# Chunked attention and two MLPs on one core: q, k and softmax weights transposed by DMA as 16-bit halves

## The chip, the cores and the metric

The kernel runs on one core of a Trainium2 chip. The metric is the device time of one execution in microseconds (us); lower is better. The core has a matrix engine (TensorE, PE in the profile; its weight loads are PEld), a vector engine (VectorE, DVE), a scalar engine (ScalarE, ACT), GpSimd (POOL) and SyncE (SP), which here issues nearly all DMAs. Each engine works through its own instructions in order and waits on semaphores for the others.

## The reference

Attention within chunks of 64 tokens for 4 batches of 8 heads (576 tokens, head size 64), then two MLPs over the 2304 tokens of width 512: one with a leaky activation (2048 hidden) and one bilinear (1536 hidden). All is float32.

```python
scores = scale * np.matmul(q_c, k_c.transpose(0, 1, 2, 4, 3))   # per chunk of 64
scores = scores - np.max(scores, axis=-1, keepdims=True)
attn = np.exp(scores)
attn = attn / (np.sum(attn, axis=-1, keepdims=True) + 1e-09)
out = np.matmul(attn, v_c)                     # then x: (2304, 512)
h = x @ w_in
x = (np.maximum(h, 0.0) + alpha * np.minimum(h, 0.0)) @ w_out
out = ((x @ w_a) * (x @ w_b)) @ w_o
```

## The kernel before, in words

Attention works on 18 groups of 128 tokens (two chunks, eight heads). A group's q, k and v are loaded with tokens on the partitions and 512 columns (`load`, L202). PE multiplies over the partitions, so k and q are first transposed by PE into PSUM, four 128x128 pieces each, and copied by ACT to the tiles kT and qT (`att_T`, L232 and L234). 32 small matmuls make the scores (`att_S`, L245). DVE subtracts the maximum (`att_M`, L258 and L260), ACT takes the exponential (`att_X`, L266), DVE divides by the sum (`att_N`, L271 to L275); the weights are in tile e. PE transposes e as well (`att_PT`, L281), ACT copies it to eT (L283), and 32 matmuls with v give the output (`att_O`, L293), which ACT and DVE split into a high and a low part, xh and xl, the first MLP's input.

Each product of the MLPs is made from such halves in three matmuls (`three`, L317). Tokens go through the first MLP in five blocks: block 0 of 512 tokens (groups 0 to 3), block 1 of 256 (groups 4 and 5), blocks 2 to 4 of 512 (groups 6 to 9, 10 to 13, 14 to 17). A block has 16 steps j: 12 matmuls into psh, the activation (`prelu`, L331: neg and pos on ACT, pos on DVE, gh on ACT, gl on DVE), and, two steps later, 12 matmuls into the accumulators acc. In block 0 the weights are also loaded, unpacked and split on ACT and DVE. The second MLP follows, block by block.

The attention of the groups of block b + 1 runs inside block b. `att_steps` (L459) gives it as a list of (slot, step); slot 2j comes between the matmuls into psh of step j and its activation, slot 2j + 1 at the end of step j (`advance` and `settle`, L600 to L633). So the attention of groups 4 and 5 runs in block 0, that of 6 to 9 in block 1, that of 10 to 13 in block 2, and that of 14 to 17 in block 3. For each block but block 1's own groups, step `turn(w)` transposes k and q of its group w, issues the loads of the next group's k and q, and transposes e of group w - 1; `multiply(w)` makes the scores of group w and the outputs of group w - 1; `soften(w)` is the exponential and the division. The steps are spread evenly over the slots.

Order is as written: every engine's instructions are issued in program order (a schedule by hand). Tiles come from pools: 72 shared tiles of 2 KB per partition (wp), 64 of which hold the first MLP's weights from block 1 on, three staging tiles of 4 KB (stg), and four PSUM banks each for accumulators and for the rest. A tile's next writer waits for the last reader of what it held.

Of the kernel before, what the change touches and what calls it, by code (L numbers as in the profile page):

```python
# [8 lines left out]
F32 = mybir.dt.float32  # L9
F32R = mybir.dt.float32r  # L10
I32 = mybir.dt.int32
U16 = mybir.dt.uint16
AF = mybir.ActivationFunctionType
# [5 lines left out]
def chunk_attention_prelu_mlp_bilinear_mlp(  # L19
# [17 lines left out]
    nc = tc.nc  # L37
    P = 128
    B, H, S, D = q.shape
    NT, DM = out.shape  # L40
# [5 lines left out]
    KD = DM // P  # L46
    J1 = F1 // P
    J2 = F2 // P
    NB = 512
    SCALE = 1.0 / float(D) ** 0.5  # L50

    sizes = [NB] + ([NT % NB] if NT % NB else []) + [NB] * (NT // NB - 1)
# [9 lines left out]
    sp = ctx.enter_context(tc.tile_pool(name="sp", bufs=3))  # L62
    st = ctx.enter_context(tc.tile_pool(name="st", bufs=4))
    dr = ctx.enter_context(tc.tile_pool(name="dr", bufs=1, space=bass.MemoryType.DRAM))
# [3 lines left out]
    def bank(nm="ps"):  # L68
        return ps_p.tile([P, DM], F32, tag="ps", name=nm)
# [5 lines left out]
    def wtile(name, dt=F32R):  # L75
        return wp.tile([P, DM], dt, tag="w", name=name)
# [88 lines left out]
    def weave(*chains):  # L165


        live, later = [], [iter(c) for c in chains]
        while live or later:
            if later:  # L170
                live.append(later.pop(0))
            live = [c for c in live if next(c, None) is not None]
# [16 lines left out]
    att = {}  # L189

    def runs(t, n):
        done = 0
        while done < n:
            b, s = divmod(t + done, S)
            step = min(n - done, S - s)
            yield done, step, b, s
            done += step

    def half(i):
        return slice(i * CH, (i + 1) * CH)  # L200

    def load(nm, u):  # L202
        a = att[nm, u] = wtile(f"{nm}{u}", F32)
        for off, n, b, s in runs(u * P, P):
            nc.sync.dma_start(
                out=a[off:off + n].rearrange("p (h d) -> p h d", h=H),
                in_={"q": q, "k": k, "v": v}[nm][b, :, s:s + n, :].rearrange("h p d -> p h d"),
            )

    def load_qk(u):  # L210
        load("k", u)
        load("q", u)

    def load_v(u):
        load("v", u)

    n_early = [0]

    def att_bank(u, nm):

        if u < sizes[0] // P:
            n_early[0] += 1
            if n_early[0] % 2:
                return acc_p.tile([P, DM], F32, tag="acc", name=nm)
        return bank(nm)

    def att_T(u, nms="kq"):
        for nm in nms:
            src = att.pop((nm, u))
            ps = att_bank(u, "psT")  # L230
            for g in range(KD):
                nc.tensor.transpose(ps[:, g * P:(g + 1) * P], src[:, g * P:(g + 1) * P], ident)  # L232
            t = wtile(f"{nm}T{u}", F32)
            nc.scalar.activation(out=t, in_=ps, func=AF.Copy)  # L234
            att[nm + "T", u] = lambda r, g, c, t=t: t[r, half(2 * g + c)]

    def att_S(u, pss=None):
        qT, kT = att.pop(("qT", u)), att.pop(("kT", u))
        pss = pss or [att_bank(u, "psS") for _ in range(2)]
        for y in range(2):  # L240
            for c in range(2):
                for e in range(2):
                    for x in (e, 1 - e):
                        i = half(e), 2 * x + y, c
                        nc.tensor.matmul(  # L245
                            out=pss[e][half(x), half(2 * y + c)], lhsT=qT(*i), rhs=kT(*i),
                            start=True, stop=True,
                        )
        att["s", u] = pss
# [15 lines left out]
    def att_X(u):  # L265
        nc.scalar.activation(out=att["e", u], in_=att["e", u], func=AF.Exp, scale=SCALE)  # L266
# [9 lines left out]

    def att_PT(u):
        e_ = att.pop(("e", u))
        ps = att_bank(u, "psP")
        for g in range(KD):  # L280
            nc.tensor.transpose(ps[:, g * P:(g + 1) * P], e_[:, g * P:(g + 1) * P], ident)  # L281
        t = wtile(f"eT{u}", F32)
        nc.scalar.activation(out=t, in_=ps, func=AF.Copy)  # L283
        att["eT", u] = t

    def att_O(u, xh, xl, col, pss=None):
        eT, v_ = att.pop(("eT", u)), att.pop(("v", u))
        pss = pss or [att_bank(u, "psO") for _ in range(2)]
        for g in range(KD):
            x, y = divmod(g, 2)  # L290
            for c in range(2):
                for e in (c, 1 - c):
                    nc.tensor.matmul(  # L293
                        out=pss[c][half(e), half(g)], lhsT=v_[half(c), half(2 * g + e)],
                        rhs=eT[half(c), half(4 * e + 2 * y + x)], start=True, stop=True,
                    )
        cols = [slice(col + c * CH, col + (c + 1) * CH) for c in range(2)]
        return [
            (xh[:, :, f], xl[:, :, f], ps[:, :KD * CH].rearrange("p (g i) -> p g i", g=KD))
            for f, ps in zip(cols, pss)  # L300
        ]

    def each(fn, parts):
        for part in parts:
            fn(*part)
# [22 lines left out]
    def s1(j, x, n):  # L328
        return proj(W["i", j], x, n)[:, :n]
# [121 lines left out]
    NU = NT // P  # L451
# [7 lines left out]
    def att_steps(b, x):  # L459

        t0, n = blocks[b]
        us = range(t0 // P, (t0 + n) // P)

        def turn(w):
            for u in us[w:w + 1]:
                att_T(u)
                if u + 1 < NU:
                    load_qk(u + 1)  # L470
            for u in us[max(w - 1, 0):w]:
                att_PT(u)
            return lambda: None

        def multiply(w):
            pss = [bank("psSO") for _ in range(2)]
            now, before = us[w:w + 1], us[max(w - 1, 0):w]
            for u in now:
                att_S(u, [ps[:, :KD * CH] for ps in pss])
            o = []  # L480
            for u in before:
                o += att_O(u, *x, u * P - t0, [ps[:, KD * CH:] for ps in pss])
                if u + 2 < NU:
                    load_v(u + 2)
            each(to_hi, o)

            def then():
                for u in now:
                    att_M(u)
                each(to_lo, o)  # L490

            return then

        def soften(u):
            att_X(u)
            return lambda: weave(att_N(u))

        def both(product):
            pss = [bank("psSO") for _ in range(2)]
            return [product(u, [ps[:, i * KD * CH:(i + 1) * KD * CH] for ps in pss]) for i, u in enumerate(us)]  # L500

        def both_S():
            both(att_S)
            return lambda: att_M(us[0])

        def both_O():
            o = sum(both(lambda u, pss: att_O(u, *x, u * P - t0, pss)), [])
            each(to_hi, o)
            for u in us:
                load_v(u + 2)  # L510
            return lambda: each(to_lo, o)

        def only(fn):
            return lambda: fn() and None or (lambda: None)

        if b == 1:
            u0, u1 = us
            return [
                (8, only(lambda: att_T(u0))),
                (10, only(lambda: (att_T(u1), load_qk(u1 + 1)))),  # L520
                (14, both_S),
                (16, lambda: lambda: att_M(u1)),
                (18, lambda: soften(u0)),
                (20, lambda: soften(u1)),
                (24, only(lambda: [att_PT(u) for u in us])),
                (27, both_O),
            ]
        steps = []
        for w in range(len(us) + 1):
            steps += [lambda w=w: turn(w), lambda w=w: multiply(w)]  # L530
            steps += [lambda u=u: soften(u) for u in us[w:w + 1]]
        last = 2 * J1 - 3
        return [(-(-last * i // (len(steps) - 1)), s) for i, s in enumerate(steps)]

    with tc.manual_schedule():
        n0 = sizes[0] // P
# [12 lines left out]
        x = xtiles("x")  # L549
# [46 lines left out]
        for b, (t0, n) in enumerate(blocks):  # L596
            nxt = xtiles("x")
            steps = att_steps(b + 1, nxt) if b + 1 < NBLK else []
# [11 lines left out]
            for j in range(J1):  # L610
# [5 lines left out]
                h = h0[0][:, :n] if not (b or j) else s1(j, x, n)  # L616
                if b == 0:
                    g = prelu_unpacking(j, h, lambda: w_dma(min(2 * j + 9, NU1)), lambda: advance(2 * j), settle)
                else:
                    rest = advance(2 * j)  # L620
                    g = prelu(j, h)
# [17 lines left out]
            x = nxt  # L639
        flush(0)  # L640

        for i, b in enumerate(order2):
            n = sizes[b]
            for j in range(J2):
                want = NU1 + max(3 * (j + 2), 20 + 2 * j)
                c = s3(j, x, n)
# [14 lines left out]
                if i + 1 < NBLK:  # L661
                    if j == J2 - 3:
                        nxt = xtiles("y")
                        halves = list(reload(order2[i + 1]))
                    if j >= J2 - 2:
                        e = j - (J2 - 2)
                        resplit(2 * e, halves[e], nxt)
            x = nxt
# [31 lines left out]
```

## Time and profile before

| | us |
|---|---|
| median of 3 runs | 912.65 (912.55 to 913.15) |
| the profiled execution | 912.5 |
| its span | 910.7 |
| PE busy | 898.5 |
| DVE busy | 403.3 |
| ACT busy | 339.4 |

Busy times are sums over the span; the three engines overlap. A stretch is read by which engine is full in it, and the chain of waits tells which instruction each one followed. Block 1 begins near 117 us of the span, block 2 near 178, block 3 near 273, block 4 near 372; the second MLP takes the part after 460.

### The profile page before, as it was taken

The numbers are of one execution on the slowest core, as the hardware profiler recorded it, in microseconds if no ns is written. First come the engines' busy times: TensorE is split into PE (matmuls) and PEld (weight loads), VectorE is DVE, ScalarE is ACT, GpSimd is POOL, SyncE is SP. The second block draws the span as 40 slices with busy tenths as digits, with TensorE's granted clock in tenths as the row PEclk, the third lists the DMA queues.
The fourth block names the chain that finished last, engine by engine and source line by source line (L and its number), as shares of the span: only waits on it lengthen the run. The fifth ranks groups of instructions, "written<-read, shape, count | busy, mean of one in ns | idle before, by whom it ended". The sixth has DMA issues, their size and how long they took to land.

```text
span 910.7 us, 13047 instructions
## 1 busy us (share of the span) xinstructions
PE 898.5 (99%) x5426; PEld 756.9 (83%) x5426; DVE 403.3 (44%) x762; ACT 339.4 (37%) x636; POOL 0.7 (0%) x6
## 2 busy tenths in 40 slices
PE   7999999999999999999999999999999999999998
PEld 6878899988888888888888888888888888888897
DVE  5999955443444343368856653111221122111222
ACT  5677654443433343356644432111211122111211
POOL 0000000000000000000000000000000000000000
PEclk9999999999999999999999999999999999999999
DMA  8685432221111110154424420200020002000100
GB/s 209 207 262 179 140 100 52 59 59 35 36 36 59 35 24 2 44 187 139 139 70 140 134 74 13 80 0 1 1 93 1 0 1 70 1 1 0 47 2 23
DMA packets 89098, 62.70 MB, mean 69 GB/s; under 512 B 59856, under 2 KB 81872, under 8 KB 89040
## 3 DMA queue, kind: packets, MB, share of 16 engines
q1 hardware_dynamic: 88752, 61.62, 22.8%
q8 instruction: 42, 0.69, 0.3%
q10 hardware_dynamic: 288, 0.26, 0.1%
q14 instruction: 16, 0.13, 0.1%
HBM read 53.49 MB, written 8.39 MB: 68 GB/s over the span
## 4 chain that ended last, share of the span: by engine, by line
PE 92%; DVE 5%; ACT 2%; issue 1%; POOLq 0%; ACTq 0%; POOL 0%; DVEq 0%
PE psh L317 52%; PE acc L317 36%; PE psT L232 1%; DVE wx L136 1%; PE psSO L245 1%; PE psP L281 1%; PE psSO L293 1%; DVE wz L128 1%; DVE wz L133 1%; DVE gl L82 0%; DVE sm L271 0%; DVE e L275 0%; PE warm L555 0%; DVE e L260 0%; DVE mx L258 0%
## 5 line engine op out<-in xcount | busy, mean ns | idle before, releaser
L393 DVE TENSOR_TENSOR b_sb<-psh,b_sb 128x512 f32<-128x512 f32 (+1 forms) x60 | 38.3, 638 | 273.2 <-PE psh L317 273.2
L337 DVE SCALAR_TENSOR_TENSOR pos<-neg,nalpha_sb,pos 128x512 f32<-128x512 f32 (+1 forms) x80 | 55.6, 695 | 116.4 <-ACT pos L336 116.2
L391 ACT ACTIVATE b_sb<-psh 128x512 f32<-128x512 f32 (+1 forms) x60 | 33.1, 552 | 167.9 <-PE psh L317 167.9
L79 ACT ACTIVATE ch<-b_sb 128x512 fp32r<-128x512 f32 (+1 forms) x60 | 35.3, 589 | 153.9 <-DVE b_sb L393 153.9
L335 ACT ACTIVATE neg<-psh 128x512 f32<-128x512 f32 (+1 forms) x80 | 44.1, 551 | 79.0 <-PE psh L317 79.0
L82 DVE TENSOR_TENSOR gl<-pos,gh 128x512 fp32r<-128x512 f32 (+1 forms) x80 | 51.0, 638 | 43.5 <-ACT gh L79 43.5
L79 ACT ACTIVATE gh<-pos 128x512 fp32r<-128x512 f32 (+1 forms) x80 | 47.3, 591 | 61.5 <-DVE pos L337 61.5
L82 DVE TENSOR_TENSOR cl<-b_sb,ch 128x512 fp32r<-128x512 f32 (+1 forms) x60 | 38.3, 639 | 39.3 <-ACT ch L79 39.3
L136 DVE SCALAR_TENSOR_TENSOR wx<-wx,wz 128x512 int32<-128x512 int32 x68 | 46.8, 688 | 4.9 <-ACT wx L124 1.0
L336 ACT ACTIVATE pos<-psh 128x512 f32<-128x512 f32 (+1 forms) x80 | 44.2, 552 | 0.0
L124 ACT ACTIVATE wx<-raw 128x512 f32<-128x512 f32 x68 | 42.7, 670 | 3.5 <-DMA raw<-in_moe_w_b_dram 3.4
L128 DVE TENSOR_SCALAR wz<-raw 128x512 uint16<-128x512 uint16 x68 | 29.7, 461 | 2.6 <-DMA raw<-in_moe_w_b_dram 2.6
L133 DVE TENSOR_SCALAR wz<-raw 128x512 uint16<-128x512 uint16 x68 | 30.9, 454 | 0.0
L234 ACT ACTIVATE kT<-psT 128x512 f32<-128x512 f32 x18 | 10.7, 594 | 20.1 <-PE psT L232 20.1
L79 ACT ACTIVATE xh<-psSO 128x256 fp32r<-128x256 f32 x28 | 9.1, 381 | 17.1 <-PE psSO L293 17.1
L266 ACT ACTIVATE e<-e 128x512 f32<-128x512 f32 x18 | 11.2, 623 | 10.4 <-DVE e L260 10.4
L281 PE MATMUL psP<-ident,e 128*128 128x128 f32 x72 | 11.6, 287 | 3.3 <-ACT eT L283 1.7
L258 DVE TENSOR_REDUCE mx<-psSO 128x4 f32<-128x256 f32 x28 | 10.5, 416 | 5.2 <-ACT xh L79 5.2
L275 DVE TENSOR_TENSOR e<-e,rc 128x512 f32<-128x512 f32 x18 | 12.4, 691 | 0.6
L271 DVE TENSOR_REDUCE sm<-e 128x8 f32<-128x512 f32 x18 | 12.2, 680 | 1.0 <-ACT e L266 0.8
L281 PEld LDWEIGHTS psP<-ident,e 128*128 128x128 f32 x72 | 8.5, 145 | 4.9 <-ACT eT L283 1.8
L232 PE MATMUL psT<-ident,q 128*128 128x128 f32 x72 | 11.2, 280 | 1.3 <-issue 1.3
(729 smaller groups left out, 2535.4 us busy)
## 6 DMA issues: line engine op xcount, KB each, us to landing
raw<-in_moe_w_out_dram SPq DMA_DIRECT2D x28, 512.0 KB, 3.5
raw<-in_moe_w_in_dram SPq DMA_DIRECT2D x16, 512.0 KB, 4.8
raw<-in_moe_w_b_dram SPq DMA_DIRECT2D x12, 512.0 KB, 4.9
raw<-in_moe_w_a_dram SPq DMA_DIRECT2D x12, 512.0 KB, 3.5
k<-in_k_dram SPq DMA_DIRECT2D x16, 256.0 KB, 3.8
q<-in_q_dram SPq DMA_DIRECT2D x16, 256.0 KB, 3.2
v<-in_v_dram SPq DMA_DIRECT2D x16, 256.0 KB, 3.3
out_dram<-os SPq DMA_DIRECT2D x8, 512.0 KB, 2.8
```

The lines of the kernel that those rows point to most:

```text
L79: nc.scalar.activation(out=hi, in_=src, func=AF.Copy)
L82: nc.vector.tensor_tensor(out=lo, in0=src, in1=hi.bitcast(F32), op=ALU.subtract)
L124: return nc.scalar.activation(out=x.bitcast(F32), in_=hw.bitcast(F32), func=AF.Copy, scale=2.0 ** -112)
L128: yield nc.vector.tensor_scalar(out=z2[:, :, 0], in0=h2[:, :, 1], scalar1=13, scalar2=None, op0=ALU.logical_shift_right)
L133: yield nc.vector.tensor_scalar(out=z2[:, :, 1], in0=h2[:, :, 3], scalar1=1 << 15, scalar2=None, op0=ALU.bitwise_and)
L136: yield nc.vector.scalar_tensor_tensor(out=x, in0=x, scalar=3, in1=z, op0=ALU.logical_shift_left, op1=ALU.bitwise_or)
L317: nc.tensor.matmul(out=ps, lhsT=a, rhs=b, start=(i == 0 and first), stop=(i == n_i - 1 and a is wl))
L335: nc.scalar.activation(out=neg, in_=h, func=AF.Relu, scale=-1.0)
L336: yield nc.scalar.activation(out=pos, in_=h, func=AF.Relu)
L337: yield nc.vector.scalar_tensor_tensor(out=pos, in0=neg, scalar=nalpha_sb[:, j:j + 1], in1=pos, op0=ALU.mult, op1=ALU.add)
L391: nc.scalar.activation(out=b_sb, in_=pb, func=AF.Copy)
L393: nc.vector.tensor_tensor(out=b_sb, in0=pa, in1=b_sb, op=ALU.mult)
```

## The change

For groups 6 to 17 k and q no longer go to PE to be transposed. `load_kq` loads both (into one staging tile, except for group 6). `apart` has ACT copy each with its 32-bit values taken apart: 512 low halves of 16 bits, then 512 high halves on each partition; and a DMA writes these to a DRAM tile, so that DRAM holds 256 rows of 512 halves, two for each token (`halves`). `turn_qk` issues a DMA that transposes the 256 rows back into a tile of 128 partitions (`turned`). The low and high half of one value come to lie side by side, so the tile is kT or qT in 32 bits. For groups 10 to 17 the softmax weights take the same way in `att_PT`, in one go: ACT's copy, the DMA to DRAM, the transposing DMA. All these DMAs are issued by SP.

The slots are now written out in tables: `m` the products, `s` the softmax, `p` the weights' transposes, `l`, `a`, `t` the loads, the taking apart and the transposes of k and q of a group further on. In block 1 outputs follow one group behind the scores, as before; in blocks 2 and 3 two groups behind, the last two groups' outputs in one step. The groups 0 to 5 keep PE's transposes.

```diff
--- before.py
+++ after.py
@@ -211,8 +211,54 @@
         load("k", u)
         load("q", u)

+    def pair(nm, staged):
+
+        if not staged:
+            return [wtile(nm, F32) for _ in range(2)]
+        a = sp.tile([P, 2, DM], F32, tag="stg", name=nm)
+        return [a[:, i] for i in range(2)]
+
+    def load_kq(u, staged=True):
+        att["kq", u] = a = pair(f"kq{u}", staged)
+        for off, n, b, s in runs(u * P, P):
+            for i, src in enumerate((k, q)):
+                nc.sync.dma_start(
+                    out=a[i][off:off + n].rearrange("p (h d) -> p h d", h=H),
+                    in_=src[b, :, s:s + n, :].rearrange("h p d -> p h d"),
+                )
+
     def load_v(u):
         load("v", u)
+
+
+
+
+
+    P_DMA = 10
+
+    def halves(src, dst, nm):
+
+        d = dst.bitcast(U16).rearrange("p (t f) -> p t f", t=2)
+        nc.scalar.activation(out=d, in_=src.bitcast(U16).rearrange("p (f t) -> p t f", t=2), func=AF.Copy)
+        rows = dr.tile([P, 2, DM], U16, name=f"rows{nm}")
+        nc.sync.dma_start(out=rows, in_=d)
+        return rows
+
+    def turned(rows, nm):
+        t = wtile(nm, F32)
+        nc.sync.dma_start_transpose(
+            out=t.bitcast(U16).rearrange("p (g r) -> p g r", g=KD), in_=rows.rearrange("p t f -> (p t) f")
+        )
+        return t
+
+    def apart(u, staged=True):
+        a, d = att.pop(("kq", u)), pair("kqd", staged)
+        att["rows", u] = [halves(a[i], d[i], f"{nm}{u}") for i, nm in enumerate("kq")]
+
+    def turn_qk(u):
+        for nm, rows in zip("kq", att.pop(("rows", u))):
+            t = turned(rows, f"{nm}T{u}")
+            att[nm + "T", u] = lambda r, g, c, t=t: t[r, half(2 * g + c)]

     n_early = [0]

@@ -276,6 +322,9 @@

     def att_PT(u):
         e_ = att.pop(("e", u))
+        if u >= P_DMA:
+            att["eT", u] = turned(halves(e_, wtile(f"ed{u}", F32), f"e{u}"), f"eT{u}")
+            return
         ps = att_bank(u, "psP")
         for g in range(KD):
             nc.tensor.transpose(ps[:, g * P:(g + 1) * P], e_[:, g * P:(g + 1) * P], ident)
@@ -463,18 +512,9 @@
         t0, n = blocks[b]
         us = range(t0 // P, (t0 + n) // P)

-        def turn(w):
-            for u in us[w:w + 1]:
-                att_T(u)
-                if u + 1 < NU:
-                    load_qk(u + 1)
-            for u in us[max(w - 1, 0):w]:
-                att_PT(u)
-            return lambda: None
-
-        def multiply(w):
+        def multiply(w, lag):
             pss = [bank("psSO") for _ in range(2)]
-            now, before = us[w:w + 1], us[max(w - 1, 0):w]
+            now, before = us[w:w + 1], us[max(w - lag, 0):max(w - lag + 1, 0)]
             for u in now:
                 att_S(u, [ps[:, :KD * CH] for ps in pss])
             o = []
@@ -495,42 +535,72 @@
             att_X(u)
             return lambda: weave(att_N(u))

-        def both(product):
+        def both(product, us):
             pss = [bank("psSO") for _ in range(2)]
             return [product(u, [ps[:, i * KD * CH:(i + 1) * KD * CH] for ps in pss]) for i, u in enumerate(us)]

         def both_S():
-            both(att_S)
+            both(att_S, us)
             return lambda: att_M(us[0])

-        def both_O():
-            o = sum(both(lambda u, pss: att_O(u, *x, u * P - t0, pss)), [])
+        def both_O(us):
+            o = sum(both(lambda u, pss: att_O(u, *x, u * P - t0, pss), us), [])
             each(to_hi, o)
             for u in us:
-                load_v(u + 2)
+                if u + 2 < NU:
+                    load_v(u + 2)
             return lambda: each(to_lo, o)

-        def only(fn):
-            return lambda: fn() and None or (lambda: None)
+        def nothing():
+            pass
+
+        def only(fn, *a):
+            def step():
+                if a[0] < NU:
+                    fn(*a)
+                return nothing
+
+            return step

         if b == 1:
             u0, u1 = us
             return [
-                (8, only(lambda: att_T(u0))),
-                (10, only(lambda: (att_T(u1), load_qk(u1 + 1)))),
+                (8, only(att_T, u0)),
+                (10, only(att_T, u1)),
+                (10, only(load_kq, u1 + 1, False)),
                 (14, both_S),
                 (16, lambda: lambda: att_M(u1)),
                 (18, lambda: soften(u0)),
                 (20, lambda: soften(u1)),
-                (24, only(lambda: [att_PT(u) for u in us])),
-                (27, both_O),
+                (21, only(apart, u1 + 1, False)),
+                (24, only(att_PT, u0)),
+                (24, only(att_PT, u1)),
+                (24, only(turn_qk, u1 + 1)),
+                (25, only(load_kq, u1 + 2)),
+                (27, lambda: both_O(us)),
+                (28, only(apart, u1 + 2)),
+                (29, only(load_kq, u1 + 3)),
+                (30, only(turn_qk, u1 + 2)),
             ]
-        steps = []
-        for w in range(len(us) + 1):
-            steps += [lambda w=w: turn(w), lambda w=w: multiply(w)]
-            steps += [lambda u=u: soften(u) for u in us[w:w + 1]]
-        last = 2 * J1 - 3
-        return [(-(-last * i // (len(steps) - 1)), s) for i, s in enumerate(steps)]
+        u = us[0]
+        if sizes[b - 1] < NB:
+            S_, lag = {
+                "m": (0, 7, 14, 21, 28), "s": (2, 9, 16, 23), "p": (6, 13, 20, 27),
+                "l": ((4, 3), (11, 4), (18, 5), (29, 6)), "a": ((1, 2), (8, 3), (15, 4), (24, 5)), "t": ((4, 2), (11, 3), (25, 4), (29, 5)),
+            }, 1
+        else:
+            S_, lag = {
+                "m": (0, 6, 12, 18), "s": (2, 8, 14, 20), "p": (4, 10, 16, 22),
+                "l": ((3, 3), (9, 4), (15, 5), (24, 6)), "a": ((1, 2), (7, 3), (15, 4), (23, 5)), "t": ((3, 2), (13, 3), (21, 4), (29, 5)),
+            }, 2
+        steps = [(slot, lambda w=w: multiply(w, lag)) for w, slot in enumerate(S_["m"])]
+        steps += [(slot, lambda w=w: soften(us[w])) for w, slot in enumerate(S_["s"])]
+        steps += [(slot, only(att_PT, us[w])) for w, slot in enumerate(S_["p"])]
+        if lag == 2:
+            steps += [(28, lambda: both_O(us[-2:]))]
+        for i, fn in enumerate((load_kq, apart, turn_qk)):
+            steps += [(slot, only(fn, u + n)) for slot, n in S_["lat"[i]]]
+        return sorted(steps, key=lambda s: s[0])

     with tc.manual_schedule():
         n0 = sizes[0] // P
```

## Rows read from the trace of the kernel before

**Rows 1.** The page: busy us (share of the span) and instructions.
```profile
PE 898.5 (99%) x5426; PEld 756.9 (83%) x5426; DVE 403.3 (44%) x762; ACT 339.4 (37%) x636; POOL 0.7 (0%) x6
```
**Rows 2.** The page: the chain that ended last, by engine.
```profile
PE 92%; DVE 5%; ACT 2%; issue 1%; POOLq 0%; ACTq 0%; POOL 0%; DVEq 0%
```
**Rows 3.** Stretches: length, busy PE, PEld, DVE, ACT, POOL; granted clock, DMA share, GB/s.
```profile
90.00:100.00 10.00, 9.61 (x47) 7.89 (x46) 9.90 (x22) 5.49 (x11) 0.00 (x0) 1.00 0.42 132
117.00:178.00 61.00, 60.38 (x691) 57.56 (x690) 32.16 (x76) 30.69 (x78) 0.00 (x0) 1.00 0.32 78
178.00:276.00 98.00, 98.00 (x700) 81.30 (x699) 39.05 (x75) 38.90 (x74) 0.00 (x0) 1.00 0.16 39
276.00:374.00 98.00, 98.00 (x689) 80.79 (x688) 39.16 (x74) 39.32 (x74) 0.00 (x0) 1.00 0.11 28
```
**Rows 4.** PE's waits, 54 to 900 us: waited for, us in total, times, longest.
```profile
PE psP L281 <- DVE e L275: 0.7, 2, 0.4
...
PE psP L281 <- ACT kT L234: 0.3, 1, 0.3
```
**Rows 5.** The chain in order of time, block 3: start, us, what.
```profile
273.36 2.72 PE psh L317 x12
276.08 0.87 PE psT L232 x8
...
296.87 0.87 PE psT L232 x8
297.74 0.44 PE psP L281 x4
298.18 2.77 PE psh L317 x12
...
303.67 0.62 PE psSO L245 x32
304.29 0.47 PE psSO L293 x32
304.76 2.95 PE psh L317 x12
...
365.25 0.62 PE psSO L293 x32
...
371.55 2.72 PE psh L317 x12
```
**Rows 6.** The same view, blocks 0 and 1.
```profile
96.16 0.63 PE psP L281 x4
...
117.16 1.43 PE psh L317 x12
...
146.86 0.63 PE psP L281 x4
...
177.70 2.75 PE psh L317 x12
```
**Rows 7.** Groups of ACT's instructions by shape: count, busy us, mean ns, idle before.
```profile
L124 ACT ACTIVATE wx<-raw 128x512 f32<-128x512 f32 x68 | 42.7, 670 | 3.5 <-DMA raw<-in_moe_w_b_dram 3.4
L234 ACT ACTIVATE kT<-psT 128x512 f32<-128x512 f32 x18 | 10.7, 594 | 20.1 <-PE psT L232 20.1
L79 ACT ACTIVATE gh<-pos 128x256 fp32r<-128x256 f32 x16 | 6.7, 417 | 11.2 <-DVE pos L337 11.2
L79 ACT ACTIVATE yh<-xr 128x1024 fp32r<-128x1024 f32 x6 | 6.3, 1044 | 0.0
```
**Rows 8.** DMA: a queue's packets, MB, share of 16 engines; issues with median us to landing.
```profile
q1 hardware_dynamic: 88752, 61.62, 22.8%
...
k<-in_k_dram SPq DMA_DIRECT2D x16, 256.0 KB, 3.8
...
x2d<-xs SPq DMA_DIRECT2D x2, 256.0 KB, 2.3
```
**Rows 9.** SP's own waits: waited for, us in total, times, longest.
```profile
SPq L205 <- PE psT L232: 77.8, 8, 13.8
```

## What the change was forecast to do

> **What bounds the kernel now.** I read the page's busy times first. The reader is to see that TensorE (PE) is busy for 898.5 of the 910.7 us of the span [rows 1], and that the chain of work that ended last lies on PE for 92% of it [rows 2]. Then the table by stretch, cut near the starts of blocks 1 to 4: in the stretches of blocks 2 and 3 PE is busy for 98.00 of 98.00 us at the full clock, in that of block 1 for 60.38 of 61.00, while ScalarE (ACT) is at 30.7 to 39.3 us and VectorE (DVE) at 32.2 to 39.2 [rows 3]. Only the end of block 0 has a second engine at its limit: DVE 9.90 of 10.00 us, ACT 5.49 [rows 3]. What PE waits for in blocks 1 to 3 comes to 0.3 us for a copy of kT and some 0.3 of the 0.7 us for the softmax weights e [rows 4]. So a PE instruction taken out of blocks 1 to 3 shortens the kernel by its own spacing, as long as nothing else arrives later than PE does now.
>
> **What one group's transposes cost.** The chain in order of time shows block 3 piece by piece, without a gap [rows 5]: 12 matmuls take 2.72 us, the eight transposes of a group's k and q 0.87, the four of its softmax weights 0.44, the scores 0.62, the outputs 0.47 behind scores (0.62 alone), and the matmuls behind a product 2.95, which is 0.23 more. From 273.36 to 371.55 it is 98.19 us. Of this 32 x 2.72 = 87.04 are the block's own matmuls; 4 x 0.87 + 4 x 0.44 = 5.24 are transposes; 4 x 0.62 + 3 x 0.47 + 0.62 + 5 x 0.23 = 5.66 are the products. The rest, 0.25, is 0.05 behind each of five transposing places (2.77 for 2.72). So a transpose costs its spacing of 0.11 us.
>
> **The change part by part.**
>
> 1. *k and q of groups 6 to 17.* Twelve times eight transposes leave PE: 12 x 0.87 = 10.44 us. Four of these twelve stand in block 1 (groups 6 to 9), four in block 2, four in block 3.
>
> 2. *Softmax weights of groups 10 to 17.* Eight times four: 8 x 0.44 = 3.52 us. Those of groups 6 to 9 stay on PE in block 1. Three of these four take 0.61 to 0.63 there already (one row stands), and the one that now follows k and q at 0.44 will begin by itself, so I charge 0.17 [rows 6].
>
> 3. *What goes with them.* The 0.05 behind ten transposing places in blocks 2 and 3 is 0.5; with block 1, where some places stay, I take 0.4. Of the 0.6 us that PE waits in block 1, the 0.3 for kT has no cause left; the wait for e is DVE's, and I leave it. Sum: 10.44 + 3.52 + 0.4 + 0.3 - 0.17 = 14.5 us.
>
> 4. *Outputs two groups behind the scores.* In blocks 2 and 3 the same products are made: four scores and four outputs in five places, the last now with two outputs (0.62 + 0.47). 0 us; PE's places only change.
>
> 5. *Copies on ACT.* 24 + 8 evacuations of 0.59 to 0.60 us go, 19.1 us. 32 copies of 1024 halves per partition come. No row has one; the nearest in element count is the 128x1024 copy at 1.04 us, so 33.4 us in all [rows 7]. The lower bound is a 512-element copy, 0.59; the upper is twice the strided copy of the weights, 2 x 0.67 = 1.34. Net +14 us on ACT, spread over blocks 0 to 3. In block 1 it means 8 x 1.04 - 8 x 0.59 = +3.6 on 30.7 of some 57 us. Each pair of copies stands ahead of a prelu and holds it for 2.1 us. PE multiplies by that prelu's result two steps later: four runs of 12 matmuls, 5.8 us in block 1 (1.44 each) and 10.9 in the other blocks, against the prelu's own five steps, of which gh at 256 columns takes 0.42 [rows 7], so some 2.3 with their hand-overs (an estimate). Cover left in block 1: 5.8 - 2.3 - 2.1 = 1.4 us. 0 us; gone, it costs up to 0.7 per group (at 1.34 each with an exp beside). In block 0 the pair for group 6 stands where DVE is full; ACT there has 4.5 of 10 us free, so 0 to 0.5, and I take 0.
>
> 6. *DMAs on SP's queue.* Per operand: the rows go out (256 KB; 2.3 us for the store of that size) and come back transposed. No row shows a transposing DMA. The nearest row by bytes is the load of k, 256 KB in 3.8 us [rows 8]. The other end follows from how finely it is cut: the queue's 88752 packets took 22.8% of 16 engines' 910.7 us, which is 37 ns each. If the 131072 halves of one operand moved in pieces of 32, 4096 pieces on 16 engines would take 9.6 us; one by one, 306 us. I take 3.8, since its pieces (256 bytes) are nearest to the 512-byte run that one destination partition receives per block of columns.
>
> 7. *The new waits.* SP waits for ACT's copy, then for the rows to have landed, before it issues a transpose. Behind it stand the next loads of k, q and v and the stores of x2d. Before, these loads stood behind PE as well, 77.8 us in total, because 64 of the 72 shared tiles hold weights [rows 9]. My count of the 8 others in program order peaks at 8 after the change too, so SP should wait no longer for a tile; the untransposed k and q move to the three staging tiles. PE waits for a transposed pair at its scores. The tightest distances: group 10, from slot 25 of block 1 to slot 0 of block 2, 7 slots; a slot there lasts (177.70 - 117.16) / 32 = 1.9 us now [rows 6] and 1.76 after, so 12.3 us. In block 2 group 13 has 5 slots of 2.9, 14.5 us. Two transposes of 3.8 need 7.6. The weights' round trip has at least 8 slots, 23 us, against 1.0 + 2.3 + 3.8 = 7.1. So hidden: 0 us. The cover is gone above some 6 us a transpose.
>
> [...]
>
> **The rivals.** *A, the transposes are the bound (slower).* They share the 16 DMA engines, so what counts is the sum. The first is issued at slot 24 of block 0, about 96 us [rows 6]; the last is needed at the outputs of group 17, some 351 us after the change (365 less 14) [rows 5]. 32 transposes in 255 us is 8 us each at best; with the distances above it decides from about 6. In pieces of 32 halves they take 32 x 9.6 = 307 us, 52 more than there is: 898 + 52 = 950 us. [...] Against: a destination partition gets 512 contiguous bytes at a time, and DMA is idle for most of these blocks (shares 0.11 to 0.32) [rows 3].
>
> *B, block 1 is too short.* Its slots are the shortest. The load of k and q of group 9 has slots 4 to 8, about 8 us, and waits first for the rows of group 8 to leave the staging tile and shares the engines with two stores of x2d. ACT waits for it in order, ahead of a prelu with 1.4 us of cover. At 2 us lost for each of groups 8 to 11, and as much again at the pairs of copies at 1.34, 4 x 2 = 8 us come back: 906 us. For it: the load's 3.8 us, 2.3 of the rows and the copies make 8.2. Against: the buffer is asked for only by SP, and ACT is half idle.
>
> *C, no change.* The time PE saves is waited elsewhere, DVE in block 1 for instance. DVE is at 32.2 of 61.0 us there, and PE would have to wait 14 us: 911 us. Little speaks for it.
>
> **How the numbers follow.** The profiled execution took 912.5 us with a span of 910.7, so 1.8 lie around it; the median of the runs, 912.65, is 0.15 above. 910.7 - 14.5 + 1.8 + 0.15 = 898.1, so I forecast 898.0. Chances: forecast (897 to 901) 0.70, B (901 to 909) 0.16, C 0.04, A 0.10. The low end takes in that all 0.7 us of PE's waits for e go and the 0.17 isn't paid, with 0.3 for the runs' spread: 898.0 - 1.2 = 896.8. The high end, 906, reaches to the price of B and leaves out A, C and a little of B. The measurement can tell about 0.2% (1.8 us) from no change: faster 0.86, same 0.04, slower 0.10.
>
> **What would show it.** Right: block 3 takes 98.2 - 5.4 = 92.8 us from its first psh to the next block's, block 2 loses as much, and block 1 lasts about 57; 48 transposes of k and q and 40 of weights remain on PE; a copy of halves takes near 1.04 us; a transpose lands within 6 us of its issue; PE's waits on kT, qT and eT come to under 1 us. Wrong, A: PE idles in blocks 1 to 3 until a DMA of kT, qT or eT, and the DMA share there is near 1. Wrong, B: PE waits for gl in block 1 while ACT waits for a load of kq or for a staging tile. What would make the whole prediction wrong is that time per transposing DMA, which no row gives.

## The result and the profile after

The changed kernel takes 897.67 us (median of 4 runs, 897.18 to 898.17) against 912.6 before: a ratio of 0.9835 (95% interval 0.9823 to 0.9848), 15 us or 1.6% less. Beside the experiments it ran twice more, at 897.79 and 897.59. The span of the profiled execution falls from 910.7 to 895.8.

The first part of the page, its DMA queue and its DMA issues, and the group of ACT's new copies (they answer to rows 1, 8 and 7):

```profile
PE 884.1 (99%) x5298; PEld 743.9 (83%) x5298; DVE 402.7 (45%) x762; ACT 352.6 (39%) x636; POOL 0.7 (0%) x6
...
L242 ACT ACTIVATE kqd<-kq 128x1024 uint16<-128x1024 uint16 x24 | 23.9, 1047 | 0.3 <-DMA kq<-in_k_dram 0.3
...
q1 hardware_dynamic: 127152, 78.41, 31.0%
...
rowsk<-kqd SPq DMA_DIRECT2D x12, 256.0 KB, 2.1
...
kT<-rowsk SPq DMA_TRANSPOSE x12, 4.0
qT<-rowsq SPq DMA_TRANSPOSE x12, 3.5
eT<-rowse SPq DMA_TRANSPOSE x8, 3.2
```

PE has 128 instructions fewer (5426 - 5298 = 96 + 32) and is busy 14.4 us less; it is still the full engine. ACT has as many as before and is busy 13.2 us more. A transposing DMA lands 3.2 to 4.0 us after its issue, by the medians of the three groups.

The waits of PE between 54 and 900 us (answers to rows 4), then the stretches from the first psh of blocks 1, 2 and 3 to that of the next (answers to rows 3; same columns):

```profile
PE psT L278 <- ACT pos L385: 0.6, 1, 0.6
PE psP L330 <- DVE e L321: 0.4, 1, 0.4
```
```profile
117.30:173.38 56.08, 56.08 (x657) 53.94 (x657) 32.00 (x76) 33.32 (x78) 0.00 (x0) 1.00 0.72 172
173.38:263.98 90.60, 90.47 (x642) 74.15 (x641) 38.17 (x75) 44.17 (x75) 0.00 (x0) 1.00 0.47 113
263.98:356.68 92.70, 92.70 (x641) 75.87 (x641) 38.91 (x75) 40.62 (x70) 0.00 (x0) 1.00 0.26 69
```

PE waits for no DMA at all; both waits that this view lists are in block 0. The DMA share of block 1 went from 0.32 [rows 3] to 0.72. The chain in order of time (answers to rows 5 and 6), start, us, what:

```profile
117.30 1.43 PE psh L366 x12
...
131.00 0.44 PE psP L330 x4
...
173.38 2.76 PE psh L366 x12
...
186.31 0.43 DVE xs L459
...
186.78 1.66 PE acc L366 x6
...
263.98 2.72 PE psh L366 x12
...
347.20 1.09 PE psSO L342 x64
...
356.68 2.72 PE psh L366 x12
```

The reader is to see that block 3 is products and matmuls alone, that the weights' transposes that stay in block 1 cost 0.44 each, and that at 186 us PE's chain runs over DVE's copy xs, which before it did not. From the first psh of each block to that of the next (before from rows 5 and 6):

| us | before | after | difference |
|---|---|---|---|
| block 1 | 60.54 | 56.08 | -4.46 |
| block 2 | 95.66 | 90.60 | -5.06 |
| block 3 | 98.19 | 92.70 | -5.49 |

With block 0 longer by 0.14 that is -14.87, the whole difference of the spans (14.9).

### The profile page after: what moved, and what is told of

Same layout as the page of the kernel before. It is cut to its first block, busy times and chain, and to the rows that moved or that the text cites. A ratio compares the mean times of both kernels' runs of the same rounds, so it can differ in the third digit from the quotient of the medians.

```text
span 895.8 us, 12893 instructions
## 1 busy us (share of the span) xinstructions
PE 884.1 (99%) x5298; PEld 743.9 (83%) x5298; DVE 402.7 (45%) x762; ACT 352.6 (39%) x636; POOL 0.7 (0%) x6
## 4 chain that ended last, share of the span: by engine, by line
PE 92%; DVE 6%; ACT 2%; issue 1%; ACTq 0%; POOLq 0%; DVEq 0%; POOL 0%
PE psh L366 52%; PE acc L366 37%; DVE wx L136 1%; PE psSO L291 1%; PE psSO L342 1%; DVE wz L128 1%; DVE wz L133 1%; DVE gl L82 0%; PE psT L278 0%; DVE sm L317 0%; PE warm L625 0%; PE psP L330 0%; DVE e L321 0%; DVE mx L304 0%; DVE e L306 0%
## 5 line engine op out<-in xcount | busy, mean ns | idle before, releaser
L242 ACT ACTIVATE kqd<-kq 128x1024 uint16<-128x1024 uint16 x24 | 23.9, 1047 | 0.3 <-DMA kq<-in_k_dram 0.3
L242 ACT ACTIVATE ed<-e 128x1024 uint16<-128x1024 uint16 x8 | 8.5, 1058 | 17.2 <-DVE e L321 13.6
L82 DVE TENSOR_TENSOR xl<-psSO,xh 128x256 fp32r<-128x256 f32 x28 | 10.2, 415 | 1.5 <-ACT xh L79 1.5
L291 PEld LDWEIGHTS psSO<-kT,qT 64*64 64x64 f32 x448 | 7.7, 134 | 3.7 <-issue 2.8
```

The lines of the kernel that those rows point to most:

```text
L82: nc.vector.tensor_tensor(out=lo, in0=src, in1=hi.bitcast(F32), op=ALU.subtract)
```

## Experiments

Throughout, the theory is the prediction's: the gain is PE's own time for the transposes, and the new way over ACT, SP and DMA is hidden by the distance between a step's slot and its use. The rivals were that the new order of the slots brings part of it, and that the way is either far cheaper or far dearer than the slots suggest. The median of the kernel before was 912.6 to 912.8 throughout.

**The order without the DMAs.** All transposes are done by PE again, in the changed kernel's slots; the copies of halves and their DMAs are gone. In the second kernel those of groups 6 and 7 are moved.

```diff
-    P_DMA = 10
+    P_DMA = 18
 def apart(u, staged=True):
-    a, d = att.pop(("kq", u)), pair("kqd", staged)
-    att["rows", u] = [halves(a[i], d[i], f"{nm}{u}") for i, nm in enumerate("kq")]
+    pass
 def turn_qk(u):
-    ...
+    att["k", u], att["q", u] = att.pop(("kq", u))
+    att_T(u)
```

> The changed kernel's slots and order, but PE transposes k, q and the weights of every group again, as before. Theory (the gain is the PE time of the transposes): 10.4 + 3.5 + 0.4 us come back, so 911.5 to 913. Rival (part of the gain comes from the new order of products, softmax and loads): the time stays below 909, by as much as the order is worth.

Measured: 921.75 us, 9 more than before. Its waits of PE, then its chain near the worst one:

```profile
PE psT L276 <- ACT pos L383: 6.2, 2, 5.5
```
```profile
102.96 1.11 PE psT L276 x4
104.08 4.33 PE acc L364 x12
```

At slot 24 of block 0 the transposes wait 5.5 us until ACT has emptied the PSUM banks, and 12 matmuls behind that take 4.33 us instead of 2.72. That could be the place and not the order, so the second kernel moves them:

```diff
-                (24, only(turn_qk, u1 + 1)),
...
-                (30, only(turn_qk, u1 + 2)),
+                (29, only(turn_qk, u1 + 1)),
+                (31, only(turn_qk, u1 + 2)),
```

> As e1_order_only, but PE transposes k and q of groups 6 and 7 at slots 29 and 31 of block 0 instead of 24 and 30, so that they no longer wait there for PSUM banks behind two groups' weights. Theory (the order is worth nothing by itself): 912 to 915, with the 5.5 us wait at the end of block 0 gone. Rival (the order itself is bad for PE transposes, not that place): it stays near 921.

Measured: 918.55 us, ratio 1.0061 (1.0046 to 1.0076); neither number was right. Its waits of PE:

```profile
PE psT L276 <- ACT pos L383: 3.1, 2, 2.5
PE psh L364 <- ACT kT L278: 1.1, 4, 0.4
```

PE still waits 2.5 us in one go at the end of block 0, and the matmuls behind run slow again. By the first psh of each block the three stretches take 59.92, 97.40 and 97.00 us, 254.3 in all; before it was 254.4, with two groups' transposes (1.74 us) more in them. So in blocks 1 to 3 the order costs about 1.7 us, of which 1.1 is PE waiting for a bank that ACT's copy of kT still holds, and the rest of the loss is block 0.

What follows: on balance none of the 15 us comes from the order. With PE's transposes this order is worse than the old one; it pays only together with the DMAs, which need no PSUM bank. One piece does belong to it. Block 1 has the transposes of four groups' k and q before and in this kernel, and here it is 0.6 us shorter (59.92 against 60.54): its four weight transposes take 0.44 us each, and PE no longer waits for e there. The 2.3 us by which blocks 2 and 3 are worse outweigh it.

**k and q alone.**

```diff
-    P_DMA = 10
+    P_DMA = 18
```

> k and q of groups 6 to 17 go by DMA, all softmax weights by PE, in the changed kernel's slots. Theory: the eight groups' weights cost 8 x 0.44 us on PE and little behind them, so 901.2 to 901.9, that is 3.5 to 4.2 over the changed kernel's 897.7. Rival (ACT's longer copies or SP's waits for the weights had a price of their own): less than 3 over it.

Measured: 902.9 us, 5.2 more than the changed kernel and more than either side had put. Blocks 1, 2 and 3 take 56.08, 93.48 and 94.64 us. Block 3 is 1.94 longer, which is 4 x 0.44 and 0.05 behind each. Block 2 is 2.88 longer: there PE's transposes of group 10 follow its softmax by two slots only and wait 1.2 us for DVE (1.6 in total with block 0's 0.4):

```profile
PE psP L330 <- DVE e L321: 1.6, 2, 1.2
```

The profiled execution (903.28 us, the longest of the four) also has block 0 longer by 0.86 us, where nothing was changed; why, no run here shows. The weights' part of the gain is the PE time forecast, plus a wait that the way by DMA, being used 8 slots later, doesn't show. For the weights, the copies on ACT and SP's waits show no price of their own; for k and q that rests on the sum of block 3.

**The distance taken away for four pairs.**

```diff
-"t": ((3, 2), (13, 3), (21, 4), (29, 5)),
+"t": ((11, 2), (17, 3), (21, 4), (29, 5)),
```

> Only the slots of four pairs of transposes move: those of groups 12 and 16 from slot 3 to 11, those of 13 and 17 from 13 to 17, one slot (2.9 us) ahead of their scores. Theory: a pair needs 1.25 + 1.25 + 3.5 = 6 us from SP's issue to landing, so PE waits some 3 us four times, 907 to 912, and the profile shows scores waiting for qT. Rival (the distance was not what hid them; PE's queue of later work covers it): no more than 1 us over the changed kernel.

Measured: 922.43 us, 24.7 more than the changed kernel. The mechanism came as expected, the size was double. Its PE waits, the chain at the first of the four places, and the stretches around the third:

```profile
PE psSO L291 <- DMA qT<-rowsq: 15.6, 4, 4.1
```
```profile
202.56 1.07 ACT ed L242
203.65 2.00 DMA rowse<-ed
...
205.70 1.23 SPq L249
...
206.97 1.30 SPq L249
...
208.32 3.65 DMA qT<-rowsq
...
212.11 0.69 PE psSO L291 x32
212.80 0.83 PE psSO L342 x32
213.63 4.14 PE acc L366 x12
```
```profile
312.00:316.00 4.00, 0.30 (x6) 0.10 (x6) 0.00 (x0) 0.00 (x0) 0.00 (x0) 0.89 1.10 192
316.00:320.00 4.00, 4.00 (x69) 3.50 (x70) 0.39 (x1) 1.64 (x4) 0.00 (x0) 0.50 0.13 30
320.00:324.00 4.00, 4.00 (x15) 3.12 (x15) 3.04 (x8) 1.26 (x2) 0.00 (x0) 0.76 0.00 0
```

Two things were missing in the expectation. The pair waits on SP behind the weights of the group before, whose rows must have been copied by ACT and landed, so it starts at 206.9 and not at its slot: PE waits 3.9 us, not 3. And behind the third wait the granted clock is 0.50 for 4 us and 0.76 over the next 4: the matmuls behind the four waits take 4.14 to 4.84 us where 2.95 is usual, and the products there up to 1.98 instead of 1.09. These are 8 to 9 us, which with the 15.6 give 24.

**Every transpose twice.**

```diff
-        nc.sync.dma_start_transpose(
+        for _ in range(2):
+            nc.sync.dma_start_transpose(
```

> Every transposing DMA is issued twice into the same tile, the second waits for the first to land, so that the way of one pair from SP to PE grows from some 6 us to some 15. Theory (it is hidden by distances of 12 to 17 us that are not much longer than needed): PE waits at the scores of group 10, perhaps also 13 and in block 1, by 2 to 4 us each, 900 to 910. Rival (DMA has far more room than the slots suggest): within 0.5 us of the changed kernel, 897.2 to 898.2. Rival A of the forecast (the stream of transposes is the bound): 32 times 3.6 us more, beyond 950.

Measured: 929.23 us, 31.6 more. PE's waits:

```profile
PE psSO L292 <- DMA qT<-rowsq: 11.7, 4, 3.6
PE psSO L343 <- DMA eT<-rowse: 5.6, 3, 4.7
PE acc L367 <- ACT gh L79: 3.4, 2, 3.1
```

Its chain at the wait for gh, and its DMA queue:

```profile
99.95 5.68 DMA kT<-rowsk
...
106.93 3.51 DMA qT<-rowsq
...
111.78 4.62 DMA raw<-in_moe_w_out_dram
```
```profile
q1 hardware_dynamic: 160944, 86.80, 35.4%
```

The rival that DMA has far more room falls, and so does my 900 to 910. What I had not counted is what stands behind a longer pair on SP. A pair now holds SP for 10 us and more. At the end of block 0 a load of the MLP's weights stands behind the first pair and goes out at 111.78 us instead of 104.40; ACT waits 7.5 us for it ahead of a prelu's gh, and PE waits 3.1 us for that. Further on it is the loads of k and q that go out late; ACT waits for them five times, 7.5 us in total. It isn't the stream as such that binds: the queue's packets take 35.4% of 16 engines' span. The room of the changed kernel is between one and two transposes per operand.

**Outputs one group behind the scores in blocks 2 and 3.**

```diff
-"m": (0, 6, 12, 18), ...
+"m": (0, 6, 12, 18, 24), ...
-            }, 2
+            }, 1
```

> The changed kernel with outputs one group behind the scores in blocks 2 and 3 (products at slots 0, 6, 12, 18, 24; the weights' DMAs where they were). Theory (two groups behind costs PE nothing and is what hides the weights' way of some 7 us, which now has two slots, 5.5 us, and the softmax in front): PE waits 3 to 6 us for eT at each of eight outputs, and at the half clock behind them for one or two more: 930 to 955. Rival (one group behind would do): within 3 us of the changed kernel.

Measured: 922.11 us, 24.5 more, below what was expected but no doubt on the side of the theory. Its waits of PE, and its chain at the first two outputs of block 2:

```profile
PE psSO L342 <- DMA eT<-rowse: 17.8, 7, 7.7
```
```profile
193.60 2.48 DMA rowse<-ed
...
199.51 1.14 PE psSO L342 x32
200.65 4.62 PE acc L366 x12
...
219.79 0.71 PE psSO L342 x32
```

I had put 3 to 6 us at each of eight outputs. Seven wait, but very unevenly: the first of block 2 for 7.7 us and the first of block 3 for 7.2, the other five for 0.2 to 1.0 each. At those two the rows of the weights stand on SP behind the stores of x2d, the loads of k and q and a pair of transposes; in block 2 they go out only at 193.60 us, when PE has been waiting since 191.8. The matmuls behind the two waits, 4.62 and 5.20 us instead of 2.95, make up most of the rest. So two groups behind hides both, the weights' way of some 7 us and what stands in front of it on SP; without the second, one group behind lacks up to 1 us at an output.

**The gap in block 2.**

```diff
-"s": (2, 8, 14, 20), "p": (4, 10, 16, 22),
+"s": (3, 8, 14, 20), "p": (5, 10, 16, 22),
```

> In blocks 2 and 3 the first softmax moves from slot 2 to 3 and its transposes from 4 to 5, so that DVE copies the accumulators of the block before (xs) ahead of the softmax's sums. Theory (the 0.4 us by which block 2 came out longer than forecast is PE's first product into acc waiting for that copy): block 2 is shorter by 0.3 to 0.5, 897.1 to 897.8, and no gap is left at the first acc of block 2. Rival (the 0.4 is something else): the gap stays.

Measured: 897.34 us (896.98 to 897.49) beside 897.79 for the changed kernel on the same chip. Its chain in block 2:

```profile
173.64 2.75 PE psh L366 x12
...
263.80 2.72 PE psh L366 x12
```

Block 2 now takes 90.16 us instead of 90.60, and the step over DVE's xs is gone. The times alone could not tell it (ratios 0.9832, 0.9815 to 0.9848, against 0.9840, 0.9825 to 0.9855), the block length does. Block 0 of this run is 0.27 us longer, which hides part of it in the span.

> The changed kernel itself, to stand beside the next ones on the same chip: 897.2 to 898.2.

Measured: 897.79 us.

**More weights by DMA.** Three kernels carry the change on into block 1. The first:

```diff
-    P_DMA = 10
+    P_DMA = 6
 # block 1
-"m": (0, 7, 14, 21, 28), "s": (2, 9, 16, 23), "p": (6, 13, 20, 27),
+"m": (0, 6, 12, 18), "s": (2, 8, 14, 20), "p": (4, 10, 16, 22),
-            }, 1
+            }, 2
```

> Block 1 also gets outputs two groups behind the scores (the same slots for products, softmax and weights as blocks 2 and 3), and the weights of groups 6 to 9 go by DMA too. Theory (each group's weights are worth 0.44 us of PE if their 7 us way fits; here it has 8 and 6 slots of 1.75 us): 4 x 0.44 = 1.8 us less than the changed kernel, 895.6 to 896.4. Rival (SP's queue in the short block is full, the new rows and transposes push those of k and q behind them): PE waits for a DMA in block 1, 898 to 905.

Measured: 904.76 us; the rival. PE waits for qT twice, 5.2 us, because SP has weights in front of each pair. The rows of group 6's weights, issued at 129.28 next to the stores of x2d, have landed only when their transpose goes out at 134.61:

```profile
129.28 0.55 SPq L244 DMA_DIRECT2D rowse<-ed  x1
134.61 1.23 SPq L249 DMA_TRANSPOSE eT<-rowse  x1
...
139.59 1.30 SPq L249 DMA_TRANSPOSE qT<-rowsq  x1
```

The second puts pairs and loads ahead of the weights (and takes the softmax of the kernel above):

```diff
 # block 1, against the first
-"m": (0, 6, 12, 18), "s": (2, 8, 14, 20), "p": (4, 10, 16, 22),
-"l": ((4, 3), (11, 4), (18, 5), (29, 6)), ... "t": ((4, 2), (11, 3), (25, 4), (29, 5)),
+"m": (0, 6, 12, 18), "s": (2, 8, 14, 20), "p": (5, 10, 16, 22),
+"l": ((3, 3), (9, 4), (15, 5), (29, 6)), ... "t": ((2, 2), (12, 3), (25, 4), (29, 5)),
```

> As e6_lag2_all, with the softmax of e7_soft3, but in block 1 SP issues the transposes of k and q of group 8 before the weights of group 6 (slots 2 and 5) and the load of group 9 before them too (slot 3), and those of group 9 after the products of slot 12. Theory (e6 lost its gain because SP's queue held the pairs behind a weights' row store that had not landed): no wait of PE for a DMA is left in block 1, and with 4 x 0.44 less on PE and e7's 0.4 it takes 895.2 to 896.2. Rival (block 1 has too little DMA time for four more round trips): PE still waits, 898 or more.

> The changed kernel itself, to stand beside the next two on the same chip: 897.2 to 898.6.

Measured: 899.87 us against 897.59 for the changed kernel on the same chip. The four executions lie apart, two at 898.2 and 898.7 and two at 901.0 and 901.3, and the profiled one is the longest. In it one wait for qT is left, 2.8 us, and the chain shows where it comes from:

```profile
129.43 6.17 DMA kq<-in_k_dram
...
135.69 0.86 ACT kqd L242
...
136.65 1.04 ACT kqd L242
```

The load of group 9's k and q takes 6.17 us beside the stores of x2d, ACT waits for it, and softmax, weights and pairs come late behind ACT. The third kernel leaves the weights of groups 6 and 7 to PE. Its other tables are those of the first kernel for block 1 and those of the moved softmax for blocks 2 and 3:

```diff
-    P_DMA = 10
+    P_DMA = 8
```

> Between the changed kernel and e6_lag2_all: block 1 has outputs two groups behind, but only the weights of groups 8 and 9 go by DMA besides those of 10 to 17 (their rows are stored after slot 16 of block 1, when the stores of x2d and most loads of k and q are done); the softmax as in e7_soft3. Theory (what failed in e6 and e8 was the first half of block 1, where SP's queue and the DMAs of four kinds meet): no wait of PE for a DMA, 2 x 0.44 = 0.9 us less than e7_soft3's 897.3, so 896.2 to 897.0. Rival (scores one or two slots earlier are themselves too early for the pairs): PE waits for qT in block 1, 898 or more.

Measured: 902.36 us; neither. No DMA is waited for, as the theory had it, but a new wait has appeared:

```profile
PE psP L330 <- DVE e L321: 3.7, 2, 3.4
```

PE's transposes of group 7 now stand two slots behind its softmax, in a block with short slots, and wait 3.4 us for it. The changed kernel leaves four slots there. None of the three is better than the changed kernel, and only the moved softmax may be, by 0.4 us.

## Why the prediction was right, step by step

The forecast was 898.0 us with a sum of 14.5 us of PE time; 897.67 was measured, and the span lost 14.9. What bounds the kernel and what was to be taken off it were right; that the total came out within 0.4 us is in part luck, since two of the smaller parts missed by 1.0 and 0.4 us in opposite directions.

*What bounds the kernel* was right. PE is the full engine after as before, and the loss of the spans is that of three blocks in which PE has next to no gaps.

*Parts 1 and 2*, 10.44 and 3.52 us, are confirmed by block 3, where nothing else plays in: 92.70 us against the 92.8 forecast, and the loss of 5.49 is 4 x 0.87 + 4 x 0.44 and the 0.25 behind the transposes. The run with k and q alone gives the second by itself, 1.94 us in block 3 for 4 x 0.44 and what goes with it.

*Part 3* was mis-sized. It came to 0.53 us; the table of blocks, less parts 1 and 2 and with the 0.44 of part 4 put back, leaves 1.49. The miss is in block 1. The four weight transposes that stay there cost 0.44 us each, not 0.61 to 0.63: before, two of the three at that price stood right behind those of k and q, where PE had just waited for the copy of kT or for e. I had charged 0.17; instead 0.55 came off. The wait for e, which I had left standing there, went too. Both belong to the new order, since PE's own transposes show them in it as well. So block 1 gave 4.46 us where the parts made it about 3.6.

*Part 4*, outputs two groups behind at 0 us, was right for the products and missed one effect of the new tables: the softmax of group 10 comes at slot 2, so that DVE works on its sums before it has copied the last accumulators of block 1, and PE's first product into acc waits. That cost 0.44 us in block 2, as the moved softmax showed. I had looked only at PE's order there; the steps that move on DVE should have had a row of their own.

*Part 5* was right: 1.047 us for a copy of 1024 halves against 1.04 from the nearest row, and no price. Block 0, for which it took 0, came out 0.14 us longer. The 0.7 us per group that it gives for copies of 1.34 us doesn't follow from its own terms (5.8 - 2.3 - 2 x 1.34 leaves 0.8, more than the 0.62 of an exp), but the sum doesn't use it.

*Part 6*: 3.8 us were taken from the load of k; measured are 3.2 to 4.0. No row before the change could decide between this and the 9.6 us of small pieces; it was a guess that came true. Of the 38400 packets that came on, 32 x 128 are rows of 2 KB; the other 34304 make 1072 for each store and transpose together. The second transposes of the doubled run add 33792, 1056 each, so a piece has 248 bytes on average (262144 / 1056) and not the 64 of 32 halves, and rival A had no ground: a transposing DMA of the changed kernel lands in 3.2 to 4.0 us, against 3.7 and 3.9 for plain loads of k of the same size in the same trace.

*Part 7* had the right answer with a reason that was too simple. All is hidden, but I measured distances from a slot to its use, as if SP issued at the slot. The experiments show that SP's queue decides: a pair goes out when the rows in front of it have landed, and loads stand behind it. The largest waits in them, 7.7 and 7.2 us, came where the weights' rows had to stand behind stores, loads and a pair. "Gone above some 6 us a transpose" was therefore roughly right in size, since twice the transpose costs 31.6 us, but it comes by way of late loads and slower matmuls too (12 in 4.16 us at 229.93 us of that run, instead of 2.95).

*Rival B* was closer than its 0.16 says. ACT did wait for the load of kq, for 0.3 us, and of the three attempts to put more into block 1 one made it true as described (ACT waited 4.5 us for the load of kq, and PE 2.8 for qT); the other two lost time to SP's queue and to PE's wait for the softmax. The price of 8 us leaves out the "as much again" of its own words; it is near what the worst of the three lost, though that was SP's queue (904.76 - 897.7 = 7).

## What to carry to other kernels

Where one engine is full from end to end, work taken off it pays its spacing in that engine's queue (0.11 us for a transpose here), not its duration (0.27). A block in which that engine never waits can be added up beforehand to a tenth of a microsecond (block 3: 92.8 against 92.70); in block 1, where it had waits, the same sum missed 0.85 us. The work that replaces it is free as long as the in-order queue that issues it, and not only its slot, lies far enough ahead of the use (with four pairs late, one went out only at 206.97 us, behind the weights of the group before, and PE waited 3.9 us for it): count what stands in front of it and behind it there. A wait of a full TensorE can cost more than its length: with four pairs late, waits of 15.6 us cost 24, because the matmuls behind them took 4.14 to 4.84 us instead of 2.95; the granted clock was 0.62 over the 3 us behind the first wait and 0.50 over the 4 us behind the third.

## What the runs showed that I had not expected

- In the changed kernel a transposing DMA occupies SP for 1.24 us to issue when nothing holds it up, a plain one of the same size for 0.36. At two per group SP is busy with it for 2.5 us, longer than PE was with the transposes (0.87 us per group).
- Behind several of PE's waits the granted clock was lower for some us. With four pairs late it was 0.62 over the 3 us behind the first wait (3.9 us), 0.86 over the next 4 and 1.00 over the 4 after these. Behind the wait of 2.5 us at the end of block 0 (the order without the DMAs, second kernel) it was 0.53 from 117.0 to 119.8 us, and 12 matmuls took 4.35 us instead of 2.72. In three other runs the matmuls were slow in the same way: 12 took 4.33 us behind 5.5 us in the first kernel of that experiment, 4.62 instead of 2.95 behind 7.7 us with outputs one group behind, and in block 1 2.31 and 2.25 instead of 1.63 behind the two waits for qT (5.2 us together) in the first kernel with more weights by DMA. Not every wait had it: in the run with every transpose twice, 12 matmuls took 2.94 us behind the wait for qT that ended at 250.8 us.
- Transposes on PE also hold PSUM banks until ACT has copied them. In the old order that cost little (0.3 us in blocks 1 to 3); in the new order, with PE's transposes, PE waited 1.1 us for such banks, and the order as a whole cost about as much as the transposes of two groups (1.7 us).
